# Beacon attention followed by a two-layer network: one pair of heads turned by DMA instead of on TensorE, and the start-up steps re-cut

## The chip, the core and the metric

The kernel runs on one core of one Trainium2 chip. The metric is the device time of one execution in microseconds (us). Before the change three runs gave 337.94, 339.75 and 342.99 us; the median is 339.75 us.

## What is computed

The inputs are `q`, `k`, `v` of shape 8 batches x 8 heads x 576 positions x 64, sixteen extra "beacon" keys and values per head, and two weight matrices of 512 x 2048 and 2048 x 512. The reference, cut to what matters:

```python
k_all = concatenate([beacon_k, k], axis=2)       # 16 + 576 keys
v_all = concatenate([beacon_v, v], axis=2)
scores = q @ k_all.T / 8                         # causal for the 576, beacons always seen
a = softmax(scores)
x = (a @ v_all)  -> (4608 tokens, 512)           # the 8 heads of a token side by side
h = x @ w_in                                     # 512 -> 2048
out = maximum(0.01 * h, h) @ w_out               # 2048 -> 512
```

## The kernel before

**Pairs and chunks.** Two neighbouring heads of one batch form a pair. There are 32 pairs, numbered g = 0 to 31, four to a batch. For each pair the queries and keys have to stand with the 64 head dimensions of both heads on the 128 partitions (tiles `qT`, `kT`). Scores are computed transposed (keys on partitions), ScalarE turns them into `aT` with an exponential, GpSimd zeroes the triangles above the diagonal, and TensorE multiplies `aT` by the values into `av`. A column of ones beside the values gives the row sums. VectorE takes their reciprocals (`rec`) and writes the normalised result to `x_nat`, with tokens on partitions. For the two-layer network the result must be turned again, so that the features stand on partitions: that is the tile `xT`, 128 x 4 pairs of a batch x 4608 tokens. The network works on nine chunks of 512 tokens. Chunk 0 needs pairs 0 to 3 alone. Chunk 1 begins in batch 0 and ends in batch 1, so it needs pairs 0 to 7.

**Two ways to turn a result.** `x_transposes` (L388) does it on TensorE: five transposes through the identity matrix `ident` into a PSUM tile, then one copy to `xT` by VectorE or ScalarE. `x_turn` (L400) does it by DMA: two `dma_start_transpose` instructions on the queue of the Sync engine (SP), one for the four full tiles of 128 tokens and one for the first 112 tokens. For a result of pair 5 both write the same columns of `xT`. The step `x` goes through `finish` (L540), which also notes how many chunks are ready; for pair 5 that number is 1 before and after.

**Two ways to turn queries and keys.** Pairs 0 to 7 are turned on TensorE (`t_q`, L223) from tiles `q_raw`, `k_raw`. From pair 8 on they are loaded by GpSimd's queue into `q_nat`, `k_nat` (step `N`, L159) and turned by two DMA transposes on SP's queue (step `T`, L169). The results go out of the core through SP's queue too (L478).

**Order.** The order on each engine is written out by hand for the first eight pairs, as strings of steps that `run` (L548) executes one by one (L617 to L625). In them `l`, `V`, `N`, `i`, `o` are loads that GpSimd issues; `q`, `k` turn queries and keys; `s2.1` is part 1 of the scores of pair 2, `m` a mask, `v5.0` the first half of the value products of pair 5, `x` and `y` the two ways to turn a result; `u` is a unit of the first layer (128 features of a chunk, four products), `d` a unit of the second (a quarter of the sum for 128 tokens, four products); `w` and `W` (L509, L521) are products of an all-zero tile `blank` whose result nobody reads. Each engine runs its own instructions strictly in this order and waits by semaphores for what it needs. From pair 8 on, a list of events with due times places the steps, and units of the network fill the gaps (L653 to L692).

**Start.** GpSimd's queue first issues the loads of pair 0 (`l0.0 l1.0`), then builds `ident` with `make_identity` (L607; a memset and a select, both on GpSimd), then issues the other loads. The masks of pairs 0, 1 and 2 stand on GpSimd behind these loads.

Of the kernel before, what the change touches and what calls it, by code (L numbers as in the profile page):

```python
# [15 lines left out]
def kernel(  # L16
# [11 lines left out]
    nc = tc.nc  # L28
# [58 lines left out]
    ident = singles.tile([128, 128], BF16, name="ident")  # L87
# [160 lines left out]
    def score(g, n):  # L248
        qT, kT = qk[g]
        if n == 0:  # L250
            probs[g] = a_bufs[g % NA]
        aT = probs[g]
        parts = SCORES[n]
        sc = ps_sc.tile([128, 2, 512], FP32, name="sc", tag="sc")
        c0 = parts[0][3]
        for c, q0, w, col in parts:
            for par in range(2):
                ps_ = slice(par * 64, par * 64 + 64)
                nc.tensor.matmul(  # L259
                    out=sc[:, par, col - c0 : col - c0 + w],  # L260
                    lhsT=kT[ps_, c * 128 : (c + 1) * 128],
                    rhs=qT[ps_, q0 : q0 + w],
                    start=True,
                    stop=True,
                    skip_group_check=True,
                )
        w = sum(p[2] for p in parts)
        nc.scalar.activation(  # L268
            out=aT[:, :, c0 : c0 + w], in_=sc[:, :, 0:w], func=AF.Exp, scale=0.125
        )  # L270
# [3 lines left out]
    def mask(g, part):  # L274
        aT = probs[g]
        for lo, n, rows in MASKS[part]:
            triangle(aT, lo, n, rows)
# [82 lines left out]
    def value_ahead(g):  # L360
        if (g, 0) not in avs:
            avs[g, 0] = ps_one.tile([128, 512], FP32, name="av", tag="one")
        value_matmuls(g, 0, avs[g, 0][:, 0:396].rearrange("p (n w) -> p n w", w=66), (0, 1))
        begun.add(g)
# [175 lines left out]
    def finish(g, eng=0):  # L540
        if eng < 2 and g in xs:
            x_transposes(g, (dve, act)[eng])
        ready[0] = chunks_with(g)
        if g % NPAIR == NPAIR - 1:
            turn[0] = 1
            held[0] = KEPT

    def run(steps):  # L548
        for step in steps.split():
            op, a = step[0], [int(x) for x in step[1:].split(".")] if step[1:] else []  # L550
            if op == "s":
                score(*a)
            elif op == "m":
                mask(*a)
            elif op == "v":
                value(*a)
            elif op == "e":
                value_ahead(*a)
            elif op == "x":
                finish(*a)  # L560
            elif op == "l":
                load_qk(*a)
            elif op == "V":
                load_v_cast(*a)
            elif op == "N":
                load_natural(*a)
            elif op == "T":
                turn_pair(a[0])
            elif op == "y":
                x_turn(a[0])  # L570
            elif op == "q" or op == "k":
                t_q(a[0], 0 if op == "q" else 1, (dve, act)[a[1] if len(a) > 1 else 0])
            elif op == "b":
                beacon_columns(a[0], (dve, act, pool)[a[1]])
            elif op == "u":
                up()
            elif op == "P":
                moe1_early(*a)
            elif op == "d":
                down()  # L580
            elif op == "w":
                unused(*a)
            elif op == "W":
                unused_ahead(*a)
            elif op == "i":
                load_w_in(a[0])
            elif op == "o":
                load_w_out(a[0])
            else:
                raise ValueError(step)  # L590
# [11 lines left out]
    with order:  # L602
        load_first_keys()
        load_beacon_k(0, 2, nc.scalar)
        nc.vector.memset(blank, 0.0)  # L605
        run("l0.0 l1.0")
        make_identity(nc, ident)  # L607
        make_ones()
        run("l1.1 l2.0 l2.1 V0.0 V0.1 l3.0 l3.1 V0.2 V0.3 V0.4 l4.0 l4.1 i0")
        make_pads()  # L610
        unused(13, 256)
        cast_beacon_k(0, 2, nc.scalar.copy)
        beacon_transposes(0, 2)
        unused(13)
        nc.scalar.copy(out=k_nat0[:, :, 0], in_=first_k[:, 0])
        nc.vector.tensor_copy(out=k_nat0[:, :, 1], in_=first_k[:, 1])
        run("q0.1 k0 w2.384 s0.0 m0.0 w3.256 s0.1 q1 s0.2 m0.1 k1 s0.3 m0.2")  # L617
        run("w2.384 s1.0 m1.0 q2 s1.1 k2 w2.384 s1.2 m1.1 w2.384 s1.3 m1.2 W0.0.4 s2.0 m2.0 W0.0.4 s2.1 W0.0.2 q3 l5.0 l5.1 s2.2 k3 w3.384 v0.0 m2.1 s2.3 i1 m2.2 W0.1.4 s3.0 m3.0 v1.0 s3.1 v0.1 s3.2 v1.1 m3.1 l6.0 l6.1 s3.3 x0.1 m3.2")
        run("v2.0 V1.0 V1.1 q4 v2.1 x1 k4.1 v3.0 v3.1 x2.1 s4.0 s4.1 x3 m4.0 V1.2 V1.3 V1.4 l7.0 l7.1 u u s4.2 s4.3 q5 k5 m4.1 m4.2 u o0 u")
        load_beacon_k(2, B, nc.gpsimd)  # L620
        run("s5.0 s5.1 m5.0 u u u s5.2 s5.3 q6 k6 m5.1 m5.2 o1 u u s6.0 s6.1 m6.0 u v4.0 u v4.1 y4 N8.0 N8.1 u s6.2 s6.3 q7 k7 m6.1 m6.2 u")
        cast_beacon_k(2, B, nc.gpsimd.tensor_copy)
        run("u v5.0 u v5.1 N9.0 s7.0 s7.1 m7.0 d x5 v6.0 v6.1 T8 d s7.2 s7.3")
        beacon_transposes(2, B)
        run("m7.1 m7.2 N9.1 u b8.2 b9.2 b10.2 b11.2 x6 v7.0 T9 v7.1 d d d N10.0 N10.1 d V2.0 V2.1 x7 T10")  # L625


        FIRST = 2 * NPAIR
        COLS = FLAT[NKB]
        TILES = (NG - FIRST) * COLS // 512  # L630

        def tile_parts(n):
            at, end, parts = 512 * n, 512 * (n + 1), []
            while at < end:
                r, lo = divmod(at, COLS)
                hi = min(COLS, lo + end - at)
                parts.append((FIRST + r, lo, hi))
                at += hi - lo
            return parts

        def block(m):
            tiles = [tile_parts(n) for n in range(3 * m, min(3 * m + 3, TILES))]
            for n, parts in enumerate(tiles):
                stretch(parts, apart=n == 0)
            for parts in tiles:
                triangles(parts)

        def has_down():
            return done2[0] // NF < done1[0] // NF

        since = 0
        events = []
        for g in range(FIRST, NG):  # L653
            if g > FIRST + 2:
                events.append((g - 2.75, 0, run, ("N%d.0" % g,)))
                events.append((g - 2.45, 0, run, ("N%d.1" % g,)))
            if g > FIRST + 2:
                events.append((g - 1.75, 0, run, ("T%d" % g,)))
            if g > FIRST + 3:
                events.append((g - 1.65, 0, run, ("b%d.2" % g,)))  # L660
            at = g + (2.05 if g % NPAIR == NPAIR - 1 else 2.25)
            events.append((at, 3, value, (g, 0)))
            events.append((at + 0.37, 4, value, (g, 1)))
            events.append((at + 0.38, 5, x_turn, (g,)))
        for m in range((TILES + 2) // 3):
            events.append((FIRST + (0.4 if m else 0.6) + 1536 / COLS * m, 2, block, (m,)))
        ends = [FIRST]
        for g in range(FIRST, NG):
            events.append((g + 3.5, 2, finish, (g, 2)))
            if g % NPAIR == NPAIR - 1:  # L670
                ends.append(g + 3.5)
        for b in range(2, B):
            for n in range(2 if b == 2 else 0, NKB):
                events.append((4 * b + (-0.4 if b == 2 else -0.9) + 0.3 * n, 6, load_v_cast, (b, n)))
        events.sort(key=lambda e: e[:2])
        first_down[0] = 4
        w, d0 = 0, done1[0] + done2[0]
        for at, _, what, args in events:
            while w + 2 < len(ends) and at > ends[w + 1]:
                w, d0 = w + 1, done1[0] + done2[0]  # L680
            todo = 2 * NF * ready[0] - KEPT - d0
            aim = d0 + todo * (at - ends[w]) / (ends[w + 1] - ends[w])
            while done1[0] + done2[0] < aim and fill():
                pass
            if what is block:
                since = done1[0] + done2[0]
            elif what is value and not has_down():
                while done1[0] + done2[0] < since + 4 and fill():
                    pass
            what(*args)  # L690
        while done2[0] < NCH * NF:
            fill()  # L692
# [30 lines left out]
```

## Time and profile before

| what | value |
|---|---|
| three runs | 337.94, 339.75, 342.99 us |
| the profiled execution | 337.94 us |
| its span, first to last instruction | 336.2 us |
| TensorE busy | 326.8 us (97%) |
| GpSimd busy | 181.1 us (54%) |
| VectorE busy | 82.5 us (25%) |
| ScalarE busy | 187.0 us (56%) |
| mean granted TensorE clock | 0.995 |
| q0, the DMA queue that GpSimd fills | 18.54 MB |
| q1, the DMA queue of SP | 20.64 MB |

The profile is of one execution; 1.74 us of its time lie outside the span. PE is TensorE, PEld its weight loads, DVE is VectorE, ACT ScalarE, POOL GpSimd, SP the Sync engine; SPq and POOLq are their queues, where DMAs are issued. L12 is line 12 of the kernel. In a line of the timeline stand the start, the length of the group, the engine, the line, the operation with output and inputs, and in brackets the idle time of the engine before it with what ended it. In a line of the windows stand the stretch, its length, each engine's busy time with its instructions in parentheses, the granted clock as a share of full speed, a figure for the load of the DMA engines, and GB/s.

### The profile page before, as it was taken

What the parts mean: (1) busy time and instruction counts of PE and PEld (TensorE: products, weight loads), DVE (VectorE), ACT (ScalarE), POOL (GpSimd) and SP (SyncE); (2) the same over time, 40 slices, a digit from 0 to 9 for tenths busy, and PEclk for the clock granted to TensorE, in tenths of its full rate; (3) what the DMA queues carried; (4) which work ended last, traced back from release to release, by engine and by line L of the source; (5) the groups of instructions that cost most, each with busy time, mean ns of one, the idle gap of its engine ahead of it and who ended that gap; (6) DMA issues with size and microseconds to landing.
All of it is one profiled execution on the core that took longest, in us unless ns stands there. A gap on an engine that the chain in (4) does not pass through costs nothing.

```text
span 336.2 us, 7448 instructions
## 1 busy us (share of the span) xinstructions
PE 326.8 (97%) x2945; PEld 170.4 (51%) x2992; DVE 82.5 (25%) x201; ACT 187.0 (56%) x312; POOL 181.1 (54%) x355
## 2 busy tenths in 40 slices
PE   8899999999999999999999999999999999999996
PEld 5465565455554555554555555545555544444444
DVE  3454354122222122311331123212221310000111
ACT  4958862777565783487338843784377206533300
POOL 8986968978987785668556965773221000000000
PEclk9979999999999999999999999999999999999999
DMA  8999999999999999999999999999310120000012
GB/s 138 137 208 174 152 200 121 182 180 133 153 150 175 168 153 153 122 117 125 128 148 134 132 105 152 160 120 122 112 51 17 50 80 33 0 31 33 31 75 81
DMA packets 151922, 39.84 MB, mean 118 GB/s; under 512 B 143008, under 2 KB 145184, under 8 KB 151888
## 3 DMA queue, kind: packets, MB, share of 16 engines
q0 software_dynamic: 99824, 18.54, 83.8%
q1 hardware_dynamic: 51648, 20.64, 35.9%
q8 instruction: 23, 0.38, 0.5%
q10 hardware_dynamic: 416, 0.20, 0.2%
q14 instruction: 11, 0.09, 0.1%
HBM read 37.22 MB, written 9.44 MB: 139 GB/s over the span
## 4 chain that ended last, share of the span: by engine, by line
PE 87%; POOL 5%; DMA 5%; issue 1%; DVE 1%; ACT 0%; DVEq 0%; POOLq 0%
PE acc L424 36%; PE acc L466 33%; PE av L351 9%; PE sc L306 5%; DMA k_nat<-in_k_dram 2%; DMA v_aug<-in_v_dram 2%; PE sc L259 2%; POOL aT L281 1%; POOL v_aug L206 1%; DMA out_dram<-osb 1%; PE tp L235 1%; POOL q_nat L163 1%; POOL k_nat L163 1%; PE tp L393 1%; POOL q_raw L151 0%
## 5 line engine op out<-in xcount | busy, mean ns | idle before, releaser
L424 PE MATMUL acc<-xT,w_in_sb 128*128 128x512 bf16 x553 | 134.6, 379 | 1.7 <-DVE osb L477 0.5
L466 PE MATMUL acc<-w_out_sb,gT 128*128 128x512 bf16 (+1 forms) x568 | 131.7, 373 | 1.5 <-issue 0.2
L431 ACT ACTIVATE gT<-acc 128x512 bf16<-128x512 f32 x144 | 83.5, 620 | 73.3 <-PE acc L424 71.6
L281 POOL TENSOR_SCALAR_AFFINE_SELECT aT<-aT 128x256 bf16<-128x256 bf16 (+2 forms) x160 | 57.6, 387 | 67.5 <-ACT aT L321 37.7
L466 PEld LDWEIGHTS <-gT 128*128 128x128 bf16 x592 | 55.2, 98 | 59.4 <-issue 1.3
L424 PEld LDWEIGHTS <-w_in_sb 128*128 128x128 bf16 x576 | 53.4, 98 | 62.6 <-issue 4.1
L321 ACT ACTIVATE aT<-sc 128x512 bf16<-128x512 f32 (+3 forms) x64 | 28.9, 521 | 48.6 <-PE sc L306 48.6
L325 ACT ACTIVATE aT<-sc 128x1024 bf16<-128x1024 f32 (+3 forms) x64 | 51.8, 893 | 0.0
L477 DVE COPY osb<-acc 128x512 f32<-128x512 f32 x35 | 24.2, 692 | 90.9 <-PE acc L466 79.3
L380 DVE RECIPROCAL rec<-av 128x6 f32<-128x6 f32 (+1 forms) x64 | 12.0, 188 | 133.3 <-PE av L351 133.3
L351 PEld LDWEIGHTS <-aT 128*128 128x128 bf16 (+1 forms) x960 | 37.0, 98 | 13.1 <-issue 1.9
L351 PE MATMUL av<-v_aug,aT 128*128 128x65 bf16 (+1 forms) x960 | 40.2, 195 | 0.5 <-POOL aT L281 0.4
L163 POOL DMA_DIRECT2D q_nat<-in_q_dram x48 | 34.9, 732 | 1.0
L206 POOL DMA_DIRECT2D v_aug<-in_v_dram x40 | 34.1, 859 | 1.7 <-DMA w_in_sb<-in_moe_w_in_dram 1.4
L163 POOL DMA_DIRECT2D k_nat<-in_k_dram x48 | 34.7, 730 | 0.5 <-issue 0.2
L381 DVE TENSOR_TENSOR x_nat<-av,rec 128x384 bf16<-128x384 f32 (+1 forms) x64 | 31.4, 491 | 2.2
L268 ACT ACTIVATE aT<-sc 128x1024 bf16<-128x1024 f32 (+3 forms) x32 | 26.2, 875 | 5.4 <-PE sc L259 5.4
L306 PE MATMUL sc<-qT,kT 64*128 64x80 bf16 (+22 forms) x384 | 21.8, 250 | 0.0
L306 PEld LDWEIGHTS <-kT 64*128 64x128 bf16 x384 | 12.7, 94 | 13.6 <-issue 11.0
L259 PE MATMUL sc<-qT,kT 64*128 64x80 bf16 (+4 forms) x96 | 10.4, 296 | 0.1
L241 DVE COPY qT<-tp 128x576 bf16<-128x576 bf16 x7 | 5.3, 757 | 13.3 <-PE tp L235 13.3
L513 PE MATMUL av<-blank 128*128 128x256 bf16 (+2 forms) x40 | 7.0, 318 | 1.1 <-DVE blank L605 1.1
(45 smaller groups left out, 68.7 us busy)
## 6 DMA issues: line engine op xcount, KB each, us to landing
out_dram<-osb SPq DMA_DIRECT2D x35, 256.0 KB, 2.4
q_nat<-in_q_dram POOLq DMA_DIRECT2D x48, 72.0 KB, 4.7
k_nat<-in_k_dram POOLq DMA_DIRECT2D x48, 72.0 KB, 5.3
v_aug<-in_v_dram POOLq DMA_DIRECT2D x24, 128.0 KB, 6.3
w_in_sb<-in_moe_w_in_dram POOLq DMA_DIRECT2D x2, 1024.0 KB, 11.9
w_out_sb<-in_moe_w_out_dram POOLq DMA_DIRECT2D x2, 1024.0 KB, 11.2
q_raw<-in_q_dram POOLq DMA_DIRECT2D x8, 144.0 KB, 7.4
k_raw<-in_k_dram POOLq DMA_DIRECT2D x7, 144.0 KB, 7.9
```

The source lines that it names most:

```text
L163: nc.gpsimd.dma_start(out=t[:, :, par], in_=(q, k)[which][b, 2 * hp + par].rearrange("(t p) d -> p t d", p=NR),)
L206: nc.gpsimd.dma_start(out=dst[lo : ROWS[c], c, :, 0:D], in_=v[b, :, OFF[c] : OFF[c] + n].rearrange("h p d -> p h d"),)
L268: nc.scalar.activation(out=aT[:, :, c0 : c0 + w], in_=sc[:, :, 0:w], func=AF.Exp, scale=0.125)
L281: nc.gpsimd.affine_select(out=view, in_=view, compare_op=ALU.is_ge, fill=0.0, base=128 - n if lo == 0 else 0, channel_multiplier=-1, patte ...
L306: nc.tensor.matmul(out=(sc[par] if apart else sc[:, par])[:, at : at + b - a], lhsT=kT[ps_, c * 128 : (c + 1) * 128], rhs=qT[ps_, q0 : q0 ...
L321: nc.scalar.activation(out=probs[g][:, par, lo:hi], in_=sc[par][:, at : at + hi - lo], func=AF.Exp, scale=0.125)
L325: nc.scalar.activation(out=probs[g][:, :, lo:hi], in_=sc[:, :, at : at + hi - lo], func=AF.Exp, scale=0.125)
L351: nc.tensor.matmul(out=avv[:, n, 0 : D + 1], lhsT=aT[0 : ROWS[c], par, a0 : a0 + 128], rhs=va[0 : ROWS[c], c, 2 * hp + par, :], start=(c = ...
L381: nc.vector.tensor_tensor(out=x_nat[:, t0:t1].rearrange("p t e d -> p (t e) d"), in0=avv[:, :, 0:D], in1=rec[:, n0:n1, None].to_broadcast( ...
L424: nc.tensor.matmul(out=acc, lhsT=w_in_cols(fc, j), rhs=xT[:, j, i * 512 : (i + 1) * 512], start=(j == 0), stop=(j == NJ - 1),)
L431: nc.scalar.activation(out=gT[i][:, fc, :], in_=acc, func=AF.Prelu, alpha=0.01)
L466: nc.tensor.matmul(out=acc, lhsT=gT[i][:, fc, t * 128 : (t + 1) * 128], rhs=w_out_sb[:, fc, half * n : (half + 1) * n], start=(fc == 0), s ...
```

## The change

Four edits, all in the part of the order that is written by hand:

- The memset of `ident` moves from GpSimd to VectorE, where it stands behind the memset of `blank`; `make_identity(nc, ident, nomemset=True)` issues the select alone.
- `W0.0.2` becomes `W0.0.6`: six products of 112 columns of zeros, not two, in front of `q3`.
- `w3.384` becomes `w4.384`: four products of 384 columns of zeros, not three, in front of `v0.0`.
- `x5` goes: the result of pair 5 is no longer turned by five TensorE transposes and a VectorE copy. `y5` stands right behind `v5.1`, in front of `N9.0`: two DMA transposes on SP's queue.

```diff
         nc.vector.memset(blank, 0.0)
+        nc.vector.memset(ident, 0.0)
         run("l0.0 l1.0")
-        make_identity(nc, ident)
+        make_identity(nc, ident, nomemset=True)
         make_ones()
...
-        run("w2.384 s1.0 m1.0 q2 s1.1 k2 w2.384 s1.2 m1.1 w2.384 s1.3 m1.2 W0.0.4 s2.0 m2.0 W0.0.4 s2.1 W0.0.2 q3 l5.0 l5.1 s2.2 k3 w3.384 v0.0 m2.1 s2.3 i1 m2.2 W0.1.4 s3.0 m3.0 v1.0 s3.1 v0.1 s3.2 v1.1 m3.1 l6.0 l6.1 s3.3 x0.1 m3.2")
+        run("w2.384 s1.0 m1.0 q2 s1.1 k2 w2.384 s1.2 m1.1 w2.384 s1.3 m1.2 W0.0.4 s2.0 m2.0 W0.0.4 s2.1 W0.0.6 q3 l5.0 l5.1 s2.2 k3 w4.384 v0.0 m2.1 s2.3 i1 m2.2 W0.1.4 s3.0 m3.0 v1.0 s3.1 v0.1 s3.2 v1.1 m3.1 l6.0 l6.1 s3.3 x0.1 m3.2")
...
-        run("u v5.0 u v5.1 N9.0 s7.0 s7.1 m7.0 d x5 v6.0 v6.1 T8 d s7.2 s7.3")
+        run("u v5.0 u v5.1 y5 N9.0 s7.0 s7.1 m7.0 d v6.0 v6.1 T8 d s7.2 s7.3")
```

## The prediction

> **What bounds the kernel now.** I read the page first: the busy times and the slices.
>
> ```profile
> PE 326.8 (97%) x2945; PEld 170.4 (51%) x2992; DVE 82.5 (25%) x201; ACT 187.0 (56%) x312; POOL 181.1 (54%) x355
> PE   8899999999999999999999999999999999999996
> PEclk9979999999999999999999999999999999999999
> DMA  8999999999999999999999999999310120000012
> ```
>
> TensorE is busy for 326.8 of 336.2 us, so the end is the sum of its work and its few stalls: anything taken off it moves the end, unless a later wait gives it back. Two more things show. The granted clock drops in one place, the third slice. And the DMA engines are at 9 tenths or more from the second slice to the twenty-eighth: a transfer put in there has to push others aside. So I looked at the place of the clock by windows and at the start by the timeline.
>
> ```profile
> 14.01:17.42 3.41, 2.18 (x53) 1.48 (x54) 1.45 (x2) 2.13 (x3) 3.41 (x12) 1.00 1.86 145
> 17.42:20.83 3.41, 3.37 (x36) 1.96 (x36) 1.51 (x4) 1.96 (x3) 3.40 (x9) 0.50 1.17 213
> 20.83:24.24 3.41, 3.41 (x96) 2.92 (x94) 2.15 (x7) 2.70 (x4) 2.26 (x5) 1.00 1.15 207
> ```
>
> For 3.41 us the clock is exactly half, right after a stretch of the same length in which TensorE was busy for 2.18 us only. The idle time in that stretch is in front of two instructions, `q3` and the rest of `v0.0`:
>
> ```profile
> 15.02 0.47 PE L235 MATMUL tp<-ident,q_raw 64*64 64x64 bf16 x18 [0.82 <-DMA q_raw<-in_q_dram]
> 17.46 0.38 PE L351 MATMUL av<-v_aug,aT 128*128 128x65 bf16 x4 [0.45 <-POOL aT L281]
> ```
>
> The first waits for a load, the second for masks on GpSimd. Last I looked at the place of pair 5: TensorE, the Sync queue and the DMA issues.
>
> ```profile
> 42.05 1.30 SPq L405 DMA_TRANSPOSE xT<-x_nat  x1
> 43.41 1.29 SPq L413 DMA_TRANSPOSE xT<-x_nat  x1
> 47.18 0.43 DVE L381 TENSOR_TENSOR x_nat<-av,rec 128x256 bf16<-128x256 f32 x1
> 48.25 0.42 PE L393 MATMUL tp<-ident,x_nat 112*128 112x112 bf16 x5
> 53.10 1.23 SPq L171 DMA_TRANSPOSE qT<-q_nat  x1
> 54.43 1.85 SPq L171 DMA_TRANSPOSE kT<-k_nat  x1
> 60.79 0.84 PE L306 MATMUL sc<-qT,kT 64*128 64x512 bf16 x12
> ```
>
> The waits of the Sync queue between 44 and 54, and the DMA issues between 54.4 and 56 (KB each left out for transposes, then us to landing):
>
> ```profile
> SPq L171 <- DMA q_nat<-in_q_dram: 8.3, 1, 8.3
> ...
> kT<-k_nat SPq DMA_TRANSPOSE x1, 5.2
> ```
>
> After the two transposes of `y4` the Sync queue stands for 8.3 us on pair 8's queries, which land at about 53.1. The turn of pair 8's keys is issued at 54.43 and lands 5.2 us later, at 59.6; the first scores of pair 8 start at 60.79. This is a slack of 1.16 us only.
>
> [...] here the mean of one is 215 ns and five of them, pipelined, take 0.42 us, which I use. [...] the two transposes of `y4` took 9.5 us (median of their window) among the loads, against 4.7 us over the whole run.
>
> **The change, part by part.** The sum is made against the profiled execution, 337.94 us, which is the fastest of the three runs; the median is 1.81 us above it. I apply the difference to the median.
>
> *The memset of `ident`.* The row on GpSimd shows 0.23 us. It stands ahead of most of the loads, and the chain of waits runs over GpSimd there until the masks end at 17.45, the ones that `v0.0` waits for. So up to 0.23 us come earlier. But that chain also holds a v load of 6.33 us, which among busy DMA engines need not end earlier. Bounds 0 and -0.23; I take -0.15. On VectorE it costs about the 0.11 us of `blank`'s memset, hidden under its 2.22 us of waiting before the first beacon copy. The select now waits for VectorE, done near 1.2 us, and runs at about 2.7; queued behind it are the loads, but the wait has ended by then.
>
> *The unread products.* Four more of 112 columns: 112 columns at the pace of the 512-column products of the steady part (4 in about 0.86 us, so 0.42 ns a column) are 0.047 us each, 0.19 us in all. They lie in the 0.82 us before `q3`. One more of 384 columns is 0.16 us; it lies in the 0.45 us before `v0.0`. Both cost nothing; without that cover, 0.35 us.
>
> *The clock.* The stretch of 14.01 to 17.42 would be busy for 2.18 + 0.35 = 2.53 us (74%), and if the masks come 0.15 us earlier, for some 2.68 us (79%). Two other stretches on the same grid stayed at full clock after being busy for 2.93 us (86%; 3.78 to 7.19) and 2.86 us (84%; 106.16 to 109.57). [...] What it is worth, from the same groups at both clocks in the timeline: two scores of 512 columns 0.61 against 0.39, two of 464 0.57 against 0.37, four of 208 0.42 against 0.30, four unread products 0.56 against 0.37, twelve value products 0.84 against 0.53, eighteen 0.89 against 0.73: 0.22 + 0.20 + 0.12 + 0.19 + 0.31 + 0.16 = 1.20 us. ScalarE waits some 0.8 us for TensorE between 18.9 and 21.7, so 0.8 is the lower end if it becomes the bound. I take -1.2 where it goes, -0.7 as a mean.
>
> *`x5` goes.* In the chain of waits its transposes hold 0.26 us of TensorE (48.41 to 48.67): -0.26. The copy on VectorE, 0.46 us, was in nobody's way, and one PSUM buffer comes free.
>
> *`y5` comes.* It waits for the product on VectorE that ends at 47.61. Behind it on the Sync queue are the output of the next `d` units and `T8`. Two issues of 1.3 us put it at 47.7 to 50.3; `T8` waits until 53.1 anyway, so the issue costs nothing, with 2.8 us of cover. `N9.0` is on GpSimd's queue and isn't held. Its readers, the units of chunk 1, start at 59.84; even at the 9.8 us that a transpose of `y4` took, it lands at 58.8. What is not free is DMA time. q1 takes 35.9% of 16 engines for 336.2 us, 120.7 us of all engines. Shared by bytes (about 147 KB of 20.64 MB) this is 0.9 us; if the outputs cost nothing, shared over 48 turns of `qT`, `kT` and 25 of `xT`, 1.65 us. I take 1.3 us. It falls between 47.7 and 53, when the loads of pair 8 are still in flight and every slice is full. So pair 8's loads can land up to 1.3 us later, and the turned keys at 59.6 + 0 to 1.3; I take half, 0.65: 60.3.
>
> *Sum.* TensorE would reach pair 8's scores at 60.79 - 0.15 - 0.7 - 0.26 = 59.7, but the keys are there at 60.3 only. So the keys come last, and the gain is 60.79 - 60.3 = about 0.5 us, with 0.1 of the start's gain on the loads themselves: **-0.6 us**, 337.3 for the profiled execution and 339.1 for the median. Behind pair 8 the turn of pair 9 is next: its keys are issued at 58.05 and land at about 63, for a block at 65.13, so it isn't late.
>
> **Rivals.**
>
> *A. The early gain is kept whole.* The clock doesn't drop, and the loads of pair 8 don't feel `y5`. For it: [...] the load falls to about 1 tenth near 54. Then -0.15 - 1.2 - 0.26 = -1.6, less what 1.16 us of slack doesn't pass: -1.3 to -1.6. Time 338.3. If slow runs of the old kernel hold more than one such drop, it could be 337.
>
> *B. Slower: pair 8 is late, and its stall costs the clock.* The transposes of `y5` take as long as those of `y4`, `T8`'s packets queue behind them, and the keys land at 61.9 or later. TensorE, early by 1.1, stands still for over 1.23 us in one window, which is the idle time that halved the clock before. The price is 1.1 us of stall and half of 3.41, 1.7 us: +2.8, so 342.5. It decides from keys at about 61.0. Against it: the DMA engines ran free near 54, so that a backlog of 1.3 us is mostly gone by then.
>
> *C. Nothing reaches the end.* The clock drops as before [...] and the gains of 0.4 us are eaten by pair 8's keys: 339.75.
>
> **How the numbers follow.** The forecast has 0.42, A 0.25, B 0.13, C 0.15; 0.05 are left for what I haven't seen. Three runs that measure no change at all can tell about 2% (6.8 us): they spread over 5 us themselves. None of the cases leaves 332.95 to 346.5, so "within 2%" has most; I leave 0.08 for faster (several drops of the clock in the slower runs, all gone, or a gain in the later DMA order) and 0.06 for slower (B with several drops). The range takes A's far end of 337 less 1, as a median of three scatters, and B's end: 336.0 to 343.0.
>
> **What would show it.** The clock of 17.42 to 20.83, or its like, at 1.00 or 0.50 decides the clock term. TensorE's wait before `v0.0` should be 0.2 us or less. The Sync queue should show two transposes at about 47 to 50, with `T8` still ended by a load of pair 8, at 52.5 to 54. The start of the first scores of pair 8 (L306) tells the sum to that point: 60.2 by my forecast, 59.2 by A, over 61.5 by B, with an idle time before it. I am wrong if that start moves by over 1 us and the end doesn't follow it, or if the end moves by more than 3 us.

## The result: slower by 1.0%

The changed kernel takes 341.84 us in the median of four runs (339.98 to 342.62), the kernel before 338.85 us. The ratio is 1.0103 with a 95% interval of 1.0064 to 1.0142. A later comparison on one chip gave 1.0086 (1.0052 to 1.0119). A time here is the median of all executions, while a ratio leaves out those over 1.5% above the fastest of their kernel, so that it isn't the quotient of the two medians beside it. The forecast was a small gain; what came is nearest to rival B. The profiled execution took 342.62 us, with a span of 340.9 us, 4.7 us longer than before. It is the slowest of the four, and the medians lie only 3.0 us apart.

The page of the kernel after: busy times, TensorE and its clock in 40 slices, and the DMA queue of SP.

```profile
PE 328.8 (96%) x2945; PEld 170.8 (50%) x2992; DVE 82.2 (24%) x201; ACT 186.9 (55%) x312; POOL 181.0 (53%) x354
PE   8999999599999999999999999999999999999996
PEclk9999999699999999999999999999999999999999
q1 hardware_dynamic: 52336, 20.80, 36.1%
```

TensorE has one new hole, in the eighth slice (59.7 to 68.2 us), and the clock drops in the same slice. The drop of the third slice is gone. The queue of SP moved 0.16 MB more.

The windows of the kernel after (stretch, length, busy times, granted clock, DMA load, GB/s), first the two stretches of the start, then the place of the hole:

```profile
14.01:17.42 3.41, 3.41 (x74) 2.35 (x72) 2.13 (x4) 2.57 (x4) 3.41 (x11) 1.00 1.76 154
17.42:20.83 3.41, 3.41 (x77) 2.66 (x75) 2.04 (x7) 3.38 (x5) 3.40 (x8) 1.00 1.14 208
...
58.40:61.80 3.40, 1.02 (x5) 0.29 (x3) 0.03 (x1) 0.60 (x1) 3.40 (x6) 1.00 1.90 153
61.80:65.20 3.40, 1.77 (x13) 0.73 (x14) 0.00 (x0) 1.09 (x3) 3.40 (x5) 0.61 2.14 137
65.20:68.60 3.40, 3.18 (x8) 1.18 (x8) 0.00 (x0) 1.96 (x3) 2.79 (x7) 0.50 1.73 203
```

The timeline of the kernel after, the Sync queue and TensorE:

```profile
45.60 1.24 SPq L405 DMA_TRANSPOSE xT<-x_nat  x1
46.88 1.25 SPq L413 DMA_TRANSPOSE xT<-x_nat  x1
56.69 1.22 SPq L171 DMA_TRANSPOSE qT<-q_nat  x1
58.01 1.22 SPq L171 DMA_TRANSPOSE kT<-k_nat  x1
...
63.43 1.48 PE L306 MATMUL sc<-qT,kT 64*128 64x512 bf16 x12 [4.01 <-DMA kT<-k_nat]
70.64 0.84 PE L306 MATMUL sc<-qT,kT 64*128 64x48 bf16 x16
```

Pair 8's queries are turned at 56.69, not 53.10. TensorE then waits 4.01 us for the turned keys, and its first scores of pair 8 start at 63.43, not 60.79. What lies between this and the second block takes 7.21 us; before it took 4.34 us (60.79 to 65.13). The difference comes from the clock: the first 6 us of that stretch, until about 69.4, now run at half clock.

A block is a group of scores from pair 8 on. The account of the two profiled executions reads, by the starts of the same instructions: the first unit of the network 24.99 against 27.04, 2.05 us early; the first block 2.64 us late; the second block 5.51 us late (70.64 against 65.13); the ninth block 4.85 us late (118.66 against 113.81), since a wait of 0.5 us for an output buffer near 106 is gone; the last block 4.85 us late (255.81 against 250.96); the span 4.7 us longer.

The loads of pair 8 show where the wait comes from. The DMA issues between 39.5 and 41 us (KB each, us to landing), first of the kernel before, then of the kernel after:

```profile
q_nat<-in_q_dram POOLq DMA_DIRECT2D x2, 72.0 KB, 12.5
```

```profile
q_nat<-in_q_dram POOLq DMA_DIRECT2D x2, 72.0 KB, 16.3
```

They are issued 0.35 us earlier than before and land 3.4 us later.

### The profile page after: what moved, and what is told of

It reads as the page before. It is cut to its first block, busy times and chain, and to the rows that moved or that the text cites. A ratio compares the mean times of both kernels' runs of the same rounds, so it can differ in the third digit from the quotient of the medians.

```text
span 340.9 us, 7452 instructions
## 1 busy us (share of the span) xinstructions
PE 328.8 (96%) x2945; PEld 170.8 (50%) x2992; DVE 82.2 (24%) x201; ACT 186.9 (55%) x312; POOL 181.0 (53%) x354
## 3 DMA queue, kind: packets, MB, share of 16 engines
q1 hardware_dynamic: 52336, 20.80, 36.1%
## 4 chain that ended last, share of the span: by engine, by line
PE 89%; DMA 7%; POOL 1%; issue 1%; ACT 1%; SPq 0%; POOLq 0%
PE acc L466 36%; PE acc L424 34%; PE av L351 8%; PE sc L306 6%; DMA w_out_sb<-in_moe_w_out_dram 4%; PE sc L259 2%; DMA kT<-k_nat 2%; DMA q_raw<-in_q_dram 1%; PE tp L235 1%; POOL aT L281 1%; PE av L513 1%; ACT aT L268 1%; PE tp L393 0%; PE av L525 0%; POOL bk_raw L177 0%
## 5 line engine op out<-in xcount | busy, mean ns | idle before, releaser
L163 POOL DMA_DIRECT2D q_nat<-in_q_dram x48 | 34.8, 731 | 3.9 <-DMA q_nat<-in_q_dram 2.6
```

What stands on the lines that cost most here:

```text
L163: nc.gpsimd.dma_start(out=t[:, :, par], in_=(q, k)[which][b, 2 * hp + par].rearrange("(t p) d -> p t d", p=NR),)
```

## Experiments

Theory 1: the two DMA transposes of pair 5 hold up the loads of pair 8 that are in flight, and TensorE waits for them. The rival: the start, 2 us shorter, brings TensorE to a place where the loads were late anyway, or made them late.

### The start alone

```diff
-... u v5.0 u v5.1 y5 N9.0 s7.0 s7.1 m7.0 d v6.0 ...
+... u v5.0 u v5.1 N9.0 s7.0 s7.1 m7.0 d x5 v6.0 ...
```

(against the changed kernel, shortened: pair 5 goes back to TensorE)

> The start of the changed kernel (ident's memset on VectorE, the five more unread products), but pair 5 turned on TensorE as before. Theory 1 (the two transposes of pair 5 hold up the loads of pair 8): those loads land as before the change, near 53, the first scores of pair 8 start at 59 to 60.3 with a wait of at most 1 us, the clock doesn't drop behind them, and the time is 336 to 338. Rival (TensorE, 2 us early, meets loads that the start itself made late): the loads land at 55 or later, TensorE waits for over 2 us, and the time is 340 or more.

Measured: 337.45 us against 337.89 us before, ratio 1.000 (0.9969 to 1.0031). Issues between 39.5 and 41 and the timeline of this run:

```profile
q_nat<-in_q_dram POOLq DMA_DIRECT2D x2, 72.0 KB, 13.0
```

```profile
60.36 0.85 PE L306 MATMUL sc<-qT,kT 64*128 64x512 bf16 x12 [1.11 <-issue]
64.70 0.84 PE L306 MATMUL sc<-qT,kT 64*128 64x48 bf16 x16
```

Pair 8's loads land as before the change (issued at 39.47 and landed at 52.5, in the kernel before at 40.02 and 52.5) and there is no half clock: the mean granted clock of this execution is 1.00. The rival falls. But the start also gives nothing that the ratio shows: TensorE stands 1.11 us in front of pair 8 and starts it at 60.36, only 0.43 us earlier than before. The profile names no releaser for this wait ("<-issue"); the turn of pair 8's keys, issued at 54.80 and 5.5 us to landing, ends at 60.3. Wait and start lie a little above the 1 us and the 59 to 60.3 that I had expected.

### The turn of pair 5 alone

```diff
-... u v5.0 u v5.1 N9.0 s7.0 s7.1 m7.0 d x5 v6.0 ...
+... u v5.0 u v5.1 y5 N9.0 s7.0 s7.1 m7.0 d v6.0 ...
```

(against the kernel before)

> The start as before; only pair 5 is turned by DMA. Theory 1: pair 8's queries land 2.5 to 3.6 us later than the 53.1 before, its turned keys at 62 to 63.4, TensorE waits 1.5 to 3 us in front of pair 8's scores; time 340 to 342. Rival (the early start is the cause): pair 8's loads land near 53.5, no wait over 0.5 us, time within 0.3% of before.

Measured: 342.60 us, ratio 1.0161 (1.0116 to 1.0206). The loads land in 16.5 us, pair 8's queries are turned at 57.46, and the waits of TensorE hold:

```profile
PE sc L306 <- DMA kT<-k_nat: 3.5, 1, 3.5
```

This edit alone makes the whole loss. It is no smaller than that of all four edits together, whose interval overlaps. One more thing: with the start of the kernel before, this execution had no drop of the clock in its start (1.00 from 14.01 to 20.83) and reached the first unit of the network at 25.31 us, where the changed start alone had 25.38. The drop that I read in the profile before was a matter of that execution.

### The turn behind pair 8's

```diff
-... v5.1 y5 N9.0 s7.0 s7.1 m7.0 d v6.0 v6.1 T8 d ...
+... v5.1 N9.0 s7.0 s7.1 m7.0 d v6.0 v6.1 T8 y5 d ...
```

(against the changed kernel)

> The changed kernel, with the turn of pair 5 moved behind the turn of pair 8 on the Sync queue. Theory 1: pair 8's queries land near 53, its keys are turned by 59.6, the wait in front of its scores is under 1 us, unless the units of chunk 1, which now read pair 5's columns soon after they are issued, wait instead; time 336 to 339. Rival (the early start is the cause): pair 8 is as late as in the changed kernel, 63.4, and the time is 341 to 342.

Measured: 343.87 us, ratio 1.0193 (1.0145 to 1.0240). The waits of TensorE:

```profile
PE acc L424 <- DMA xT<-x_nat: 3.7, 1, 3.7
```

Pair 8's loads are on time again: they land in 13.0 us, and its queries are turned at 54.44. The cause holds, my time doesn't: a wait of 3.7 us now stands in front of the units of chunk 1, which read pair 5's columns. Their turn was issued at 57.03 and 58.33 and took 5.5 us to land. I had named that reader and still put the time at 336 to 339.

### The clock behind the wait

```diff
+        events.append((FIRST + 0.6, 1, unused, (25, 384)))
         ends = [FIRST]
```

(against the changed kernel: 25 unread products of 384 columns in front of the first block)

> The changed kernel with 25 unread products of 384 columns (4.0 us) in front of the first block, in the place of the 4.0 us wait. If the half clock behind the wait costs 2 to 3 us of the loss: the start of pair 8's scores stays at 63.4 to 63.8, the clock stays at 1.00 from 62 to 70, and the time is 339 to 340. If the clock costs nothing beyond the wait: as the changed kernel, 341.5 to 342.

Measured: 341.66 us (four executions: 340.61, 341.54, 341.79 and 345.92), ratio 1.0175 (1.0093 to 1.0257). The profiled execution:

```profile
62.99 0.84 PE L306 MATMUL sc<-qT,kT 64*128 64x512 bf16 x12
67.33 0.84 PE L306 MATMUL sc<-qT,kT 64*128 64x48 bf16 x16
```

With TensorE kept busy the clock stays at 1.00 from 60 to 72 us and the second block follows after 4.34 us, as in the kernel before. So in the profiled execution the half clock costs 7.21 - 4.34 = 2.87 us. The time of the kernel as a whole is not better for it; it lies in the range I had set for a clock that costs nothing beyond the wait. I repeated the pair on one chip.

> The changed kernel as it stands, on the same chip as the run after it: 340.5 to 342.5, slower than before by 0.7 to 1.4%, pair 8's scores at 62.5 to 64 behind a wait of 3 to 4.5 us.

Measured: 340.60 us, ratio 1.0086 (1.0052 to 1.0119).

> The changed kernel with 25 unread products of 384 columns in front of the first block, beside the run before it. If the half clock behind the wait costs the end its 2 to 3 us: 338.5 to 340, 0.5 to 0.9% below the run before. If what comes later takes it back (pair 9 and 10 are late as well): less than 0.3% below it.

Measured: 342.03 us, ratio 1.0141 (1.0097 to 1.0185). The kept-warm kernel isn't faster than the changed one; it came out 0.4% above it, where I had set either 0.5 to 0.9% or less than 0.3% below. Its products took 4.2 us in both profiled executions, and the wait that they fill isn't always that long: 4.01 and 3.09 us in the two profiled executions of the changed kernel. Of the fourteen executions of the changed kernel in this comparison, twelve stand in its ratio, and they show both cases: seven had a mean granted clock of 0.994 or 0.995 and a median of 341.39 us, five had 0.999 or more and a median of 338.98 us. (Of the four in the result above, the two at 1.00 took 339.98 and 342.42 us.) So in this comparison the loss is about 1.5 us over the 337.45 of before where the clock holds and about 4 us where it drops. How much of the 2.4 us between the two groups is the clock, and how much a longer wait that also brings the drop, these runs don't separate.

### Which of the two transposes, and is it the bytes?

Three kernels with the changed start and pair 5 turned on TensorE. In the place of `y5` each issues transfers from `x_nat` into a spare tile that nobody reads:

```diff
+    spare = singles.tile([128, 640], BF16, name="spare")
...
+# the four full tiles of 128 tokens:
+        nc.sync.dma_start_transpose(
+            out=spare[:, 112:624].rearrange("c (t r) -> c t r", r=128),
+            in_=x_nat[:, 1:5].rearrange("r t e d -> r (t e d)"))
+# or the first 112 tokens:
+        nc.sync.dma_start_transpose(out=spare[:, 0:112], in_=x_nat[0:112, 0].rearrange("r e d -> r (e d)"))
+# or both, as ordinary copies:
+        nc.sync.dma_start(out=spare[:, 128:640], in_=x_nat[:, 1:5].rearrange("r t e d -> r (t e d)"))
+        nc.sync.dma_start(out=spare[0:112, 0:128], in_=x_nat[0:112, 0].rearrange("r e d -> r (e d)"))
```

> The kernel with the changed start alone, pair 5 turned on TensorE, and beside it the larger of the two DMA transposes (four tiles of 128 tokens) into a spare tile that nobody reads, in the place of pair 5's turn. Theory 1a (the delay goes by the bytes turned): pair 8's first load lands in 15.3 to 15.9 us, not 13.0, TensorE waits 2.5 to 3.5 us in front of pair 8's scores, time 340 to 341.5. Rival 1b (the delay goes by the number of transposes): about half of the 3.4 us, 14.5 to 14.8 us, time 339 to 340.

> As the run before it, but only the smaller transpose (112 tokens) into the spare tile. By the bytes (1a): 0.4 to 0.8 us later than 13.0 us, time within 0.3% of before. By the number (1b): 14.5 to 14.8 us, time 339 to 340.

> As the run before it, but in place of the transposes two ordinary copies of the same bytes, issued on the Sync queue, into the spare tile. If any 147 KB put there hold up the loads: pair 8's first load lands at 15.5 to 16.5 us as in the changed kernel, time 340 to 342. If it is the turning that is dear: under 13.8 us, time within 0.3% of before.

Measured: 341.45 us, ratio 1.0113 (1.0046 to 1.0179), with the four tiles; 338.37 us, 1.0002 (0.9979 to 1.0026), with the 112 tokens; 339.68 us, 1.0017 (0.9981 to 1.0054), with the copies. The issues between 39 and 41, in this order:

```profile
q_nat<-in_q_dram POOLq DMA_DIRECT2D x2, 72.0 KB, 14.6
```

```profile
q_nat<-in_q_dram POOLq DMA_DIRECT2D x2, 72.0 KB, 13.5
```

```profile
q_nat<-in_q_dram POOLq DMA_DIRECT2D x2, 72.0 KB, 12.3
```

Against 13.0 us for the start alone, the four tiles add 1.6 us, the one tile 0.5 us, and the same bytes as ordinary copies nothing. The loads behind the weights, with the turn of pair 4 alone ahead of them, landed in 12.5 to 13.3 us in four profiled executions of this study, so the 0.5 us is hardly clear of their scatter. The times decide: each of the two transposes is one instruction, and the larger costs 1.1%, the smaller nothing that its interval shows. So in these runs the cost went by the amount turned, not by the number of instructions. The landing of 14.6 us by itself would not say so. It is less than the 15.3 that I had expected at least, and lies in the range I had given to the rival. The waits of TensorE in front of pair 8 don't tell the two apart either (2.17 and 1.95 us).

The bytes alone aren't the cost: the forecast had it that any transfer put in there pushes others aside, and with the copies pair 8's loads still landed in 12.3 us. But the copies also went in fewer packets: SP's queue had 272 more than with the start alone, with `y5` 688 more. Whether the turning itself is dear or the number of small packets that it takes, no run here separates. The two parts make 2.1 us where both transposes together made about 3 us (landings of 15.0 to 16.5 us in five runs with `y5` and the weights ahead of pair 8); with one profiled execution each, I leave that difference open.

### One turn ahead of pair 8, or none

```diff
-... v4.1 y4 N8.0 N8.1 u s6.2 ...
+... v4.1 N8.0 N8.1 u x4 s6.2 ...
```

Against the start alone this leaves no DMA turn ahead of pair 8; against the changed kernel it leaves only that of pair 5.

> The changed start, and pairs 4 and 5 both turned on TensorE, so that no transpose runs by DMA before pair 8. Theory 1: pair 8's first load lands in 9.5 to 11 us, no wait in front of its scores, which start at 58.7 to 59.5; time 335.5 to 337, faster than before by 0.3 to 0.7%. If the load of the second half of the output weights in front of it is what holds pair 8: it lands in 12.5 to 13.0 us as with pair 4 turned by DMA, and the time is that of before within 0.3%.

Measured, with none: 338.21 us, ratio 1.0014 (0.9982 to 1.0046). No gain, where I had expected 335.5 to 337. Its profiled execution took 344.55 us, far above the median, so no landing is read from it.

> The changed kernel with pair 4 turned on TensorE, so that pair 5 is the only one turned by DMA ahead of pair 8. Theory (two turns in flight ahead of pair 8's loads are one too many, whichever pair): pair 8's first load lands in 12 to 13.8 us, the wait in front of its scores is under 1.5 us, time within 0.4% of the kernel before. Rival (the later place of pair 5's turn, nearer to the end of those loads, is what hurts): they land in 15 us or more, time 340 to 342.

Measured, with pair 5's turn alone: 338.72 us, ratio 1.0014 (0.9985 to 1.0043). Its profiled execution took 341.88 us, so here too only the time is used. The turn of pair 5 costs nothing that can be seen when it is the only one. In these runs it is the second turn ahead of pair 8 that is too much (1.0103 with both, 1.000 with pair 4's alone), whichever of the two pairs it belongs to; the later place isn't the cause.

### Pair 8's loads ahead of the weights

```diff
-... s5.2 s5.3 q6 k6 m5.1 m5.2 o1 u u ... y4 N8.0 N8.1 u s6.2 ...
+... s5.2 s5.3 q6 k6 m5.1 m5.2 u u ... y4 N8.0 N8.1 o1 u s6.2 ...
```

(against the changed kernel: the load of the second half of the output weights, 1 MB, goes behind those of pair 8)

> The changed kernel with the load of the second half of the output weights (1 MB) put behind pair 8's loads on GpSimd's queue. If the queue in front of pair 8's loads is what makes them late: they land in 8 to 11 us, the scores of pair 8 no longer wait for turned keys; the third unit of the second layer waits 1 to 4 us for the weights instead; time 338 to 341. If the transposes delay those loads wherever they stand: over 14 us, time 340.5 to 342.5.

Measured: 341.14 us, ratio 1.0108 (1.0087 to 1.0130). The issues and the waits of TensorE:

```profile
q_nat<-in_q_dram POOLq DMA_DIRECT2D x2, 72.0 KB, 9.8
```

```profile
PE acc L466 <- DMA w_out_sb<-in_moe_w_out_dram: 3.9, 1, 3.9
```

Pair 8 is early with both turns in their places, so the second case, over 14 us wherever its loads stand, is out. The time is just above the 338 to 341 of the first. The wait now stands in front of the second layer, for the weights. They are issued at 41.73, not 38.56, and land in 13.4 us, in the changed kernel in 13.5. So this wait comes from their own later issue of 3.2 us, as the wait behind the moved turn comes from the later turn. What the two runs show is that moving a transfer behind another made its own reader wait for 3.7 to 3.9 us. That the DMA engines have too much to do between 39 and 57 us, so that any order has one that waits, is my reading and isn't shown.

### Where a lead of TensorE goes

```diff
-    opool = ctx.enter_context(tc.tile_pool(name="opool", bufs=2))
+    opool = ctx.enter_context(tc.tile_pool(name="opool", bufs=3))
```

> Pairs 4 and 5 turned on TensorE with the changed start, and three output buffers instead of two. Theory: a lead of TensorE is taken back near 105 by the wait for an output buffer (0.5 to 1.4 us in the profiles so far), which the third buffer takes away: no wait of TensorE on the copy to the output buffer, time 335.5 to 337, faster by 0.3 to 0.7%. Rival: the lead is taken back elsewhere (the first block, later loads): within 0.3% of before.

> The changed start alone (pair 4 by DMA, pair 5 on TensorE) with three output buffers instead of two. Theory: the first block stays bound by pair 8's loads (scores at 60 to 60.8), the wait near 105 goes; 0 to 0.3% faster than before. Rival: the output buffers are no bound: no difference.

Measured: 336.26 us, ratio 0.9975 (0.9957 to 0.9993), with pairs 4 and 5 both on TensorE; 336.74 us, 0.9979 (0.9962 to 0.9996), with the start alone. Both are a little faster than the kernel before and so than the changed one, the first by 0.25%, just under the 0.3 to 0.7% that I had expected. They don't differ from each other beyond their intervals. In both profiles the wait for an output buffer near 105 is gone; it had been 0.5 us before the change and 1.0 to 1.4 us in the runs with a spare transfer. But the profile of the start alone with two buffers doesn't have it either, so the profiles don't show that the buffer made the gain. How much the buffer alone is worth isn't told, since the kernel before wasn't run with three.

The first of the two also shows pair 8's loads with no DMA turn ahead of them:

```profile
q_nat<-in_q_dram POOLq DMA_DIRECT2D x2, 72.0 KB, 10.7
```

With none the loads land in 10.7 us, with one turn in 12.5 to 13.3, with two in 15.0 to 16.5. So the turn of pair 4 delays them too, by some 2 us in this one profile. The scores of pair 8 start at 59.84 without a wait, but this lead isn't kept: TensorE waits 0.36 us at 105.43 for an `xT` turned by DMA, and the ninth block starts at 112.72, as with the start alone. In the second too the scores start without a wait, at 61.22, though I had expected pair 8's loads to bind there.

## The prediction, step by step

**The cost of `y5` in DMA time** is the step that failed. The forecast says: "I take 1.3 us. ... I take half, 0.65". With `y5` the loads of pair 8 took about 3 us longer to land (15.0 to 16.5 us against 12.5 to 13.3), so the wait in front of pair 8 was 4.01 us, where the forecast's own sum leaves 0.6 (59.7 to 60.3). Two errors are in it. I priced the turn from the share of engine time that its queue takes over the whole run. That share can't price one turn: for the changed kernel it makes 36.1% of 340.9 us in one profiled execution and 34.8% of 342.0 us in another, 123.1 and 119.0 us, and without `y5` 116.3 to 120.7 us in three. And I set half of the price against the load that waits, as if the delay were shared out. The load paid more than the whole of it. A row of the profile shows that this load was not late by the mean load of the engines: the DMA row of the kernel after between 53 and 58 us, 40 slices of 0.125 us.

```profile
DMA  9999901101103999999999999999999999999999
```

Between 53.6 and 54.6 us the engines are idle or at a tenth while pair 8's queries, issued at 39.67, are still missing. They land at about 56. Why the rest is so slow, the profile of whole DMAs can't say. I had read the same dip near 54 in the kernel before as free capacity in which a backlog would drain, and used it against rival B.

**What comes late next.** The slack of 1.16 us at pair 8's keys was read rightly, and so was the order of the Sync queue: `y5` was issued at 45.60 and 46.88, `T8` still waited 8.5 us for its load, and the issue cost nothing. Right too was that pair 5's columns land ahead of chunk 1 in that place.

**The clock.** The drop in the start is gone in the profiled execution, and TensorE reached the network 2.05 us earlier, more than the 0.85 us I had counted for both terms. But it was no gain to be had in the median: the start alone gives 1.000. The kernel before ran 142 times beside the experiments. Nine executions had a mean clock of 0.995 or less and a median of 339.32 us, the other 133 had 0.998 or more and a median of 337.45. So a drop, wherever it lay, went with 1.9 us, more than the 1.2 that I had set, but a drop is there in one execution of sixteen only. I had taken the one that was profiled for the usual one. The 0.7 us that I took as a mean was an estimate: a chance of about 60% that the drop goes, times 1.2 us, with the chance read from three stretches of 3.41 us (busy for 64% ahead of half clock, for 84 and 86% ahead of full clock). That the busy share decides, they don't show. The sum did name pair 8's keys as the limit, so that this term hardly entered the forecast. What it left out is a half clock behind the wait at pair 8: 2.87 us in the profiled execution.

**The memset and the unread products.** The select ran at 2.73, not 2.94, and the masks at 13.59, not 13.70: 0.11 us on that chain. The wait in front of `q3` is gone. At pair 8 both vanish in the longer wait.

**`x5`.** It wasn't measured by itself. The forecast names 0.42 us for its five transposes on TensorE (one took 215 ns in the mean) as the figure it uses and then takes 0.26 us; either lies ahead of a wait that is longer.

**Rival B** had the place and what follows: keys after 61.0, a stall, the clock halved by it. I gave it 0.13. Its first step was another: the packets of `T8` would queue behind those of `y5`. But the turn of pair 8's keys landed in 5.3 us against 5.2 before; it was issued 3.6 us later, since the loads were late. Its sizes were too small: 1.1 us of stall against 2.64 measured at the first block, 1.7 us of clock against 2.87. That its 342.5 us came so near to 341.84 is in part luck. In the two profiled executions the loss is 4.7 us and not 2.8, and the 2.8 was added to a median of 339.75 us, where four executions now give 338.85. The half clock lasted 6.8 us, from about 62.6 to 69.4, not the 3.41 us that I had counted.

## To carry to other kernels

A transfer put in where the DMA engines are full can be paid by the one load whose reader has the least slack. Here that load paid about 3 us, where my estimate from shares had said 0.65. So look for that reader first, and price a DMA transpose from a run that has one more of it and not from its bytes. Before counting a gain on the busiest engine, ask what it meets next: with the start alone, the lead of 1.66 us at the first unit (25.38 against 27.04) was 0.43 us behind the wait for pair 8's keys. And before counting a loss seen in one profile, look how often it comes: a clock drop, of which the start's is one, was there in one execution of sixteen.

## What the runs showed of the hardware

- With two DMA transposes of together 147 KB put ahead of them, loads in flight landed in 15.0 to 16.5 us, not 12.5 to 13.3; with ordinary copies of the same bytes from the same queue at the same place in 12.3.
- In three profiled executions the clock can be set beside how busy TensorE was. Before the change, 3.41 us in which it was busy for 2.18 us (64%) were followed by 3.41 us at 0.50. In the changed kernel, 3.41 us in which it was busy for 0.22 us (59.20 to 62.61) were followed by 6.8 us at 0.50; it was busy for 2.44 us (72%) of the first half of these and for 3.33 us (98%) of the second, and from 69.43 the clock was 1.00. With the wait filled by unread products it stayed at 1.00 (60 to 72 us).
- The mean load of the DMA engines fell to a tenth while a load issued 14 us earlier was still outstanding: the row of 53 to 58 us above, with pair 8's queries issued at 39.67.
